# A transformer block: front loads held until x is there, roots on ScalarE, and a last tail that reads its sums from the banks

## The chip, the cores and the metric

The kernel runs on one core of a Trainium2 chip. The metric is the device time of one execution in microseconds (us); smaller is better. Engines are named as in the profile: PE (TensorE's matmuls), PEld (its weight loads), DVE (VectorE), ACT (ScalarE), POOL (GpSimd) and SP (SyncE, which issues most DMAs). A bank is one eighth of PSUM, the memory that matmuls write: 128 partitions of 512 fp32 numbers.

## The reference

One block with adaptive layer norm, for x of 2048 tokens by 512, 32 heads of 16, and an MLP of 1376; all in bf16:

```python
mod = (silu(c) @ w_mod).reshape(1, 6, 1, 512)
sa, ca, ga, sb, cb, gb = (mod[:, i] for i in range(6))
h = layernorm(x) * (1 + ca) + sa              # eps 1e-5
q, k, v = split_heads(h @ wqkv)
x = x + ga * (softmax(q @ k.T / 4) @ v merged @ wo)
h = layernorm(x) * (1 + cb) + sb
x = x + gb * (gelu(h @ w1 + b1) @ w2 + b2)
```

## The kernel before

The tokens are four blocks of 512. The attention is cut into 32 quads: quad (b, t) is four heads (t of 8) for the queries of block b. For each quad, 16 tiles of 128 keys times four heads give 64 score items, each one matmul into a bank (L949). Most go in units of three and two banks, by turns (pools psA and psB), through one exp on ACT (L1001); key tiles 3, 7, 11 and 15 go through DVE instead, as 16-bit integers whose bits are read as fp16 (L1067, L1088). The value products (`do_pv`, L1144) sum a quad in one bank (`od`, pool psO), four matmuls side by side in column groups; `do_fill` (L1165) adds products with zeros where PE would be idle. Pools ptA and ptB hold four exp results of each kind.

At a quad's end `do_out` (L1172) copies the bank to memory (`o_sb`, L1176), sends the row of sums over DRAM to `dall` and, as reciprocals (L1193), back as `rb`; POOL multiplies (L1201) and gives the tile OT. The last quad of all takes no trip: shuffle, reciprocal, multiply on DVE (L1185 to L1187).

**Front (L117 to L373).** Two DMA queues (SP and ACT) are given all loads at once: c, x of block 0 (`xb[0]`), the modulation weights W_m0, parts of W_k and W_q, the other blocks of x, W_v, the rest. `silu_c` computes silu(c); DVE takes the sums of block 0 (`ln_stats`, L201), aggregates them (L209) and finds 1/sqrt(var + eps) by shift, subtraction and two Newton rounds (`ln_rstd`, L203 to L229: nine small instructions); `ln_norm` (L232) writes the normalized rows. PE meanwhile does 13 matmuls of zeros (`warm_up`), the modulation columns (L246) and four more, then transposes (L237). `hT_evac` (L272) applies shift and scale; the first k and q products follow, and q's evacuation on DVE (L305).

**Middle.** The order of everything between is written out by a planner in the program: at each step of a planned clock every engine takes the next thing that is ready by planned durations. Side work (layer norm, projections, modulation, o-projection, MLP of finished blocks) stands in a list of jobs `job(at, rows, needs, label, hold)`: `at` is the due time in quads, `rows` are (engine, planned us, function), `needs` are labels that must have been set, and `hold` says up to which row the job keeps one of the two spare banks (pools psX0 and psX1, `aux`), which DVE's score tiles use too. Each engine executes its own instructions in the order in which the planner recorded them.

`tail_jobs(b)` (L564) is what follows attention for blocks 0 to 2: x is loaded again (`begin`), `oproj` sums eight products OT by W_o_pad in a bank (L586), DVE multiplies by ga (L592), POOL adds x (L595), then layer norm, up, gelu on ACT, down (L653), multiplication by gb and POOL's addition (L663).

**Last tail (L676 to L755).** For block 3 it starts when the attention pools are closed: eight banks `fb` for four tiles `po[tt]`, 32 products (L695), then by halves of 256 tokens `norm_half` (multiply by ga L702, add x L704 or on POOL L707, sums, `ln_rstd`, rows), `transposes`, `up_half` (44 matmuls L727, 11 gelus L729), at the end `range_flag`, one product that tells whether any softmax sum left its range (then a general path runs; not here), and four `down_tile` (L734, L736) with DVE's multiply (L739), add (L741) and the store (L742):

```python
norm_half(0)
transposes(0)
norm_half(1)
up_half(0)
transposes(1)
up_half(1)
bad, onec, fl = range_flag()
...
for tt in range(4):
    down_tile(tt)
```

Of the kernel before, what the change touches and what calls it, by code (L numbers as in the profile page):

```python
# [58 lines left out]
WARM = (13, 4)  # L59
# [30 lines left out]
def adaln_block(ctx: ExitStack, tc: tile.TileContext, A_x, A_wqkv, A_wo, B_x, B_w1, B_b1, B_w2, B_b2,  # L90
# [26 lines left out]
    wm_v = w_mod.rearrange("(j p) n -> p j n", p=P)  # L117
# [22 lines left out]
    nc.sync.dma_start(out=W_v, in_=wqkv_v[:, :, 2 * D:3 * D])  # L140
    for b in range(2, NQB):
        nc.sync.dma_start(out=xb[b], in_=x_tok[b])
    nc.sync.dma_start(out=W_k[:, :, 256:D], in_=wqkv_v[:, :, D + 256:2 * D])
    nc.sync.dma_start(out=W_q[:, :, 256:D], in_=wqkv_v[:, :, 256:D])
    W_m1 = load_mod(1, (nc.sync,))
# [18 lines left out]
    nc.vector.tensor_scalar(out=qmask, in0=pmask, scalar1=Q_SCALE, scalar2=None, op0=ALU.mult)  # L164
    magic = const.tile([P, 12], I32, name="magic")
# [64 lines left out]

    def ln_norm(src, dst, mv, rs, t, i):
        nc.vector.tensor_scalar(out=dst[:, t, :], in0=src[:, t, :], scalar1=mv[:, i, 0:1],  # L232
                                scalar2=rs[:, i:i + 1], op0=ALU.subtract, op1=ALU.mult)
# [30 lines left out]
    def second_mod_mm(ps):  # L264
        mod_cols(ps, W_m1, D, 0)
        mod_cols(ps, W_m2, 0, 4)
# [65 lines left out]
    def ln1(blocks):  # L332
        n = 4 * len(blocks)
        st = pron.tile([P, 12, 6], FP32, name="st1")
        for i in range(n):
            ln_stats(xb[blocks[i // 4]], st, i % 4, i)
        return st

    def ln1_norm(blocks, st):
        mv, rs = ln_rstd(st, 4 * len(blocks))  # L340
        for i, b in enumerate(blocks):
            for t in range(4):
                ln_norm(xb[b], xb[b], mv, rs, t, 4 * i + t)
            hn_t[b] = xb[b]

    with tc.tile_pool(name="pps", bufs=1, space=PSUM) as pps0, \
# [3 lines left out]
        st0 = ln1([0])  # L350
# [21 lines left out]
        q_proj(ps, 0, 0)  # L372
        q_evac(ps, 0, 0)  # L373
# [12 lines left out]
    NA, NB = UNIT  # L386
    att = ExitStack()
    psA = att.enter_context(tc.tile_pool(name="psA", bufs=1, space=PSUM))
    psB = att.enter_context(tc.tile_pool(name="psB", bufs=1, space=PSUM))
    psO = att.enter_context(tc.tile_pool(name="psO", bufs=1, space=PSUM))  # L390
# [5 lines left out]

    banks = [att.enter_context(tc.tile_pool(name=f"psX{i}", bufs=1, space=PSUM)) for i in range(2)]
# [20 lines left out]
    st_of = {}  # L418
# [58 lines left out]
    for b in range(1, NQB):  # L477
        at = 0.25 * (b - 1)
        def stats(j, b=b, t=0):
            if t == 0:  # L480
                st_of[b] = pron.tile([P, 12, 6], FP32, name="st1")
            ln_stats(xb[b], st_of[b], t, t)
        job(at - 0.16, [(DVE_, V_EVAC, lambda j, b=b, t=t, f=stats: f(j, b, t)) for t in range(4)],
# [23 lines left out]
    job(4.5, [(DVE_, 2.2, load_wo)], (), "wo")  # L507
# [11 lines left out]
    def row_job(at, dst, W, col0, label):  # L519
        proj_job(at, lambda ps, js: mod_row(ps, W, col0, js), lambda ps: nc.vector.tensor_copy(out=dst, in_=ps),  # L520
                 ["silu"], label)

    row_job(5.3, ga_b, W_m1, 0, "ga")
    row_job(5.5, gb_b, W_m2, D, "gb")
# [39 lines left out]
    def tail_jobs(b):  # L564
# [15 lines left out]
        def oproj(tt):  # L580
            def f(part):
                def g(j):
                    if part == 0:
                        j.ps = j.alloc()
                    for t in (2 * part, 2 * part + 1):
                        nc.tensor.matmul(out=j.ps, lhsT=OT[(b, t)][:, tt * P:(tt + 1) * P], rhs=W_o_pad[:, t, :],  # L586
                                         start=(t == 0), stop=(t == 7))
# [11 lines left out]
            job(p0 + 0.5 + 0.25 * tt, [(PE_, 2 * MM, f(i)) for i in range(4)]  # L599
                + [(DVE_, V_EVAC, mul), (POOL_, 1.2, res), (DVE_, V_EVAC, stats)],  # L600
                ["wo", ("begin", b)] + [("ot", b, t) for t in range(8)] + ([("o", b, tt - 2)] if tt > 1 else []),
# [44 lines left out]
        def down(tt):  # L646
# [18 lines left out]
            job(p0 + 4.9 + 0.5 * tt, [(PE_, (3 if i == 0 else 1 if i == 5 else 2) * MM, f(i)) for i in range(6)]  # L665
# [6 lines left out]
    for b in range(NQB - 1):  # L672
        tail_jobs(b)
    jobs.sort(key=lambda o: o.at)

    def last_tail():  # L676
# [4 lines left out]
        xr = tl.tile([P, 4, D], BF16, name="xr")  # L681
        nc.sync.dma_start(out=xr, in_=x_tok[b])
        x1 = xr
# [5 lines left out]
        with tc.tile_pool(name="fps", bufs=8, space=PSUM) as fps:  # L689
            def bank(dt=FP32, n=512):  # L690
                return fps.tile([P, n], dt, name="fb")
            po = [bank() for _ in range(4)]
            for t in range(8):
                for tt in range(4):
                    nc.tensor.matmul(out=po[tt], lhsT=OT[(b, t)][:, tt * P:(tt + 1) * P], rhs=W_o_pad[:, t, :],  # L695
                                     start=(t == 0), stop=(t == 7))
# [716 lines left out]
```

## Time and profile before

| What | Value |
|---|---|
| time, median of 3 runs | 824.18 us (823.38 to 824.9) |
| time of the profiled execution | 826.04 us |
| its span on the core | 824.3 us, 18344 instructions |
| PE busy | 781.8 us (95%), 7518 matmuls |
| DVE busy | 734.2 us (89%) |
| ACT busy | 750.6 us (91%) |
| POOL busy | 74.3 us (9%) |
| mean granted PE clock | 0.988 |
| first exp starts | 18.68 us |
| last exp ends | 778.49 us |
| last attention copy starts | 779.03 us |
| last DVE result ends | 820.24 us |

Times in the profile count from the span's start. A line of the timeline gives start, length, engine, source line, operation, result and operands with their sizes, how many instructions are merged, and in brackets how long the engine was idle before and what ended that wait. A matmul's own length (380 ns for 512 columns) is longer than the distance to the next one, since they are pipelined. A stage table gives busy times by engine in a stretch, the clock that PE was granted (1.00 is full, 0.50 half), and the share and rate of the DMA engines.

### The profile page before, as it was taken

How to read it: one execution, taken by the hardware profiler on the slowest of the kernel's cores; microseconds unless marked ns; L12 is line 12 of the kernel's file. 1: busy time of each engine (PE TensorE's matmuls, PEld its weight loads, DVE VectorE, ACT ScalarE, POOL GpSimd, SP SyncE). 2: the span in 40 equal slices, each digit the busy share in tenths (PEclk: the TensorE clock that was granted, in tenths of full speed). 3: DMA queues.
4: the chain of work that ended last, by engine and by line, in shares of the span. 5: the costliest groups of instructions: out<-in, count | busy, mean ns of one | idle time of the engine just before them, and what ended most of it. 6: DMA issues, size and time to landing. Idle time of an engine off the chain costs nothing. (4 is left out here: it accounts for less than half of the span.)

```text
span 824.3 us, 18344 instructions
## 1 busy us (share of the span) xinstructions
PE 781.8 (95%) x7518; PEld 238.0 (29%) x7518; DVE 734.2 (89%) x1324; ACT 750.6 (91%) x669; POOL 74.3 (9%) x68
## 2 busy tenths in 40 slices
PE   6999999999999999999999999999999999999967
PEld 3332222322222222222223222222223222222343
DVE  6969989999999899989989999989998999888673
ACT  2798999999999999999989999999999999999732
POOL 0000010000011000111021000011012000111010
PEclk8999999999999999999999999999999999999989
DMA  9100000113100000001100000000100000000000
GB/s 286 47 1 15 16 16 10 43 49 109 41 15 15 15 15 16 21 16 28 44 4 17 15 16 15 22 18 18 40 16 15 16 16 15 8 28 22 16 26 29
DMA packets 30667, 24.51 MB, mean 30 GB/s; under 512 B 13841, under 2 KB 24434, under 8 KB 30578
## 3 DMA queue, kind: packets, MB, share of 16 engines
q1 hardware_dynamic: 28978, 22.23, 9.5%
q8 instruction: 61, 1.00, 0.5%
q10 hardware_dynamic: 1600, 1.05, 0.4%
q14 instruction: 28, 0.23, 0.1%
HBM read 20.65 MB, written 2.61 MB: 28 GB/s over the span
## 5 line engine op out<-in xcount | busy, mean ns | idle before, releaser
L1001 ACT ACTIVATE pA<-sA 128x1536 bf16<-128x1536 f32 x310 | 467.1, 1507 | 16.0 <-PE od L1144 8.2
L1067 DVE TENSOR_SCALAR t<-aux 128x512 int16<-128x512 f32 x500 | 329.1, 682 | 29.0 <-PE aux L949 27.2
L1001 ACT ACTIVATE pB<-sB 128x1024 bf16<-128x1024 f32 x309 | 335.1, 1084 | 5.7 <-PE sB L949 2.5
L1088 DVE TENSOR_SCALAR t<-t 128x2048 int16<-128x2048 int16 x375 | 263.6, 725 | 2.1 <-PE od L1144 0.5
L949 PE MATMUL aux<-qm,kT 32*128 32x512 bf16 x500 | 175.2, 380 | 4.1 <-DVE t L1067 2.1
L949 PEld LDWEIGHTS <-kT 32*128 32x128 bf16 x2048 | 77.2, 91 | 270.6 <-issue 265.2
L1144 PE MATMUL od<-pA,VE 128*32 128x512 bf16 x930 | 143.3, 385 | 0.2 <-DVE o_sb L1176 0.2
L1144 PE MATMUL od<-pB,VE 128*32 128x512 bf16 x618 | 142.3, 386 | 0.0
L1144 PE MATMUL od<-t,VV 128*32 128x512 f16 x1500 | 139.4, 385 | 1.4 <-DVE t L1088 1.0
L949 PE MATMUL sA<-qm,kT 32*128 32x512 bf16 x930 | 123.2, 383 | 11.0 <-ACT pA L1001 8.6
L949 PE MATMUL sB<-qm,kT 32*128 32x512 bf16 x618 | 120.7, 383 | 2.9 <-ACT pB L1001 2.5
L1201 POOL TENSOR_TENSOR OT<-o_sb,rb 128x512 bf16<-128x512 f32 x31 | 41.3, 1332 | 526.1 <-DMA rb<-d 354.2
L1165 PE MATMUL od<-hT,zeros 128*32 128x512 bf16 x940 | 83.1, 385 | 0.0
L1144 PEld LDWEIGHTS <-VE 128*32 128x32 bf16 x2048 | 50.7, 94 | 98.1 <-issue 85.0
L1144 PEld LDWEIGHTS <-VV 128*32 128x32 bf16 x1500 | 39.9, 95 | 55.7 <-issue 46.9
L1144 PE MATMUL od<-t,VE 128*32 128x512 f16 x500 | 49.2, 384 | 1.3 <-DVE o_sb L1176 1.2
L628 PE MATMUL aux<-h2T,W 128*128 128x512 bf16 x132 | 39.7, 384 | 0.8 <-DVE t L1067 0.7
L653 PE MATMUL aux<-W,uG 128*128 128x512 bf16 x132 | 37.7, 383 | 0.0
L1165 PEld LDWEIGHTS <-zeros 128*32 128x32 bf16 x972 | 23.9, 95 | 36.4 <-issue 29.2
L1176 DVE COPY o_sb<-od 128x512 f32<-128x512 f32 x32 | 21.9, 684 | 8.0 <-issue 7.6
L633 DVE TENSOR_SCALAR uG<-aux,b1c 128x512 bf16<-128x512 f32 x33 | 24.4, 739 | 2.7 <-PE aux L628 2.6
L586 PE MATMUL aux<-W_o_pad,OT 128*128 128x512 bf16 x96 | 26.4, 382 | 0.2 <-DVE t L1067 0.2
(128 smaller groups left out, 417.3 us busy)
## 6 DMA issues: line engine op xcount, KB each, us to landing
rb<-d SPq DMA_DIRECT2D x124, 64.0 KB
W_m<-in_w_mod_dram SPq DMA_DIRECT2D x2, 1024.0 KB
xr<-in_A_x_dram SPq DMA_DIRECT2D x4, 512.0 KB
out_dram<-ob SPq DMA_DIRECT2D x16, 128.0 KB
xb<-in_A_x_dram SPq DMA_DIRECT2D x3, 512.0 KB
W<-in_B_w_dram SPq DMA_DIRECT2D x1, 1376.0 KB
W<-in_B_w_dram SPq DMA_DIRECT2D x1, 1280.0 KB
W_m<-in_w_mod_dram SPq DMA_DIRECT2D x1, 512.0 KB
```

The lines of the kernel that those rows point to most:

```text
L586: nc.tensor.matmul(out=j.ps, lhsT=OT[(b, t)][:, tt * P:(tt + 1) * P], rhs=W_o_pad[:, t, :], start=(t == 0), stop=(t == 7))
L628: nc.tensor.matmul(out=j.ps, lhsT=late["W_1"][:, c, fc * P:(fc + 1) * P], rhs=T["h2"][:, c, :], start=(c == 0), stop=(c == NC - 1))
L633: nc.vector.tensor_scalar(out=T["u"][:, fc, :], in0=j.ps, scalar1=late["b1c"][:, fc:fc + 1], scalar2=None, op0=ALU.add)
L653: nc.tensor.matmul(out=j.ps, lhsT=T["u"][:, fc, tt * P:(tt + 1) * P], rhs=late["W_2"][:, fc, :], start=False, stop=(fc == NFC - 1))
L949: nc.tensor.matmul(out=dst, lhsT=kT[32 * r:32 * r + 32, ch, kt * P:(kt + 1) * P], rhs=qm[(b, ch)][32 * r:32 * r + 32, par, :], start=True, ...
L1001: nc.scalar.activation(out=pt[:, 0:n, :], in_=st[:, 0:n, :], func=ACT.Exp, scale=math.log(2.0) / STEP)
L1067: nc.vector.tensor_scalar(out=t0[(qi, kt)][:, r, :], in0=sd, scalar1=T_BIAS, scalar2=0.0, op0=ALU.add, op1=ALU.max)
L1088: nc.vector.tensor_scalar(out=t16, in0=t0[(qi, kt)], scalar1=float(MJ[j]), scalar2=None, op0=ALU.add)
L1144: nc.tensor.matmul(out=od[qi][32 * r:32 * r + 32, :], lhsT=w, rhs=src, start=first, stop=last_)
L1165: nc.tensor.matmul(out=dst[32 * r:32 * r + 32, :], lhsT=zeros, rhs=hT[:, r, 0:512], start=bank is not None, stop=bank is not None)
L1176: nc.vector.tensor_copy(out=o, in_=od[qi])
L1201: nc.gpsimd.tensor_tensor(out=OT[(b, t)], in0=o, in1=j.rb, op=ALU.mult)
```

## The change

Four things, in the words of the code.

1. Front. x and c are loaded first, c and W_m0 with neighbouring rows in one partition; W_m0 follows. All other loads move to `later_loads`, on SP's queue alone. It is called after the first of block 0's sums and begins with a one-element memset of W_k on DVE: the load of W_k, and all behind it in SP's queue, wait for that memset. The root for block 0 is taken by ACT (`ln_sqrt`) and inverted by DVE; an exp of one column after it brings ACT's exp table back. `warm_up` has 18 matmuls ahead of the modulation and none behind. Three of the four sums of block 1 are taken ahead of q's evacuation.
2. Residual and ga. W_o_pad is multiplied by ga once, on POOL, in eight pieces. The o-projection of blocks 0 to 2 begins with a product of the identity and x, which adds the residual in the bank; DVE then copies the sum. The multiplication by ga and POOL's addition go. The due times of the down products are 0.6 apart instead of 0.5.
3. End of attention. The last quad's shuffle, reciprocal and multiply read the bank, and the copy that feeds the range check comes behind them. The last block's x is loaded before the end, and the o-projection of its first two tiles, up to the seventh of eight products, is made by two jobs that hold both spare banks, once DVE's score tiles are done (`d_done`).
4. Last tail. Only five banks (those of psA and psB) are taken anew; the others are used where they are. Filler matmuls (5 and 18) stand around the last products. Sums are taken from the banks, ACT copies them to x1, the first half's root is ACT's; tables are loaded by one-column instructions (`early`); `down_tile(0)` moves ahead of `up_half(1)`; the last down tile is made and stored in two halves.

The same, cut (unchanged parts and the renaming that follows from it left out):

```diff
-WARM = (13, 4)
+ST1 = 3
+WARM = 18
+KEEP = (5, 18)
...
-    wm_v = w_mod.rearrange("(j p) n -> p j n", p=P)
+    wm_v = w_mod.rearrange("(p j) n -> p j n", p=P)
...
-    nc.scalar.dma_start(out=cc_bf, in_=c.rearrange("o (j p) -> p (o j)", p=P))
     for k, eng in enumerate(two):
         eng.dma_start(out=xb[0][:, 2 * k:2 * k + 2, :], in_=x_tok[0][:, 2 * k:2 * k + 2, :])
+    nc.scalar.dma_start(out=cc_bf, in_=c.rearrange("o (p j) -> p (o j)", j=NC))
     W_m0 = load_mod(0, two)
-    nc.sync.dma_start(out=W_k[:, :, 0:256], in_=wqkv_v[:, :, D:D + 256])
-    nc.scalar.dma_start(out=W_q[:, :, 0:256], in_=wqkv_v[:, :, 0:256])
-    nc.sync.dma_start(out=xb[1], in_=x_tok[1])
...
+    def later_loads():
+        nc.vector.memset(W_k[0:1, 0, 0:1], 0.0)
+        nc.sync.dma_start(out=W_k[:, :, 0:256], in_=wqkv_v[:, :, D:D + 256])
+        nc.sync.dma_start(out=W_q[:, :, 0:256], in_=wqkv_v[:, :, 0:256])
+        nc.sync.dma_start(out=xb[1], in_=x_tok[1])
+        nc.sync.dma_start(out=W_v, in_=wqkv_v[:, :, 2 * D:3 * D])
...
+        mods[1] = load_mod(1, (nc.sync,))
...
+    def ln_sqrt(st, n):
+        mv = small.tile([P, 12, 2], FP32, name="mv")
+        for t in range(n):
+            nc.vector.bn_aggr(out=mv[:, t, :], in_=st[:, t, :])
+        rs = small.tile([P, 12], FP32, name="rs")
+        nc.scalar.activation(out=rs[:, 0:n], in_=mv[:, 0:n, 1], func=ACT.Sqrt, bias=eps_c)
+        nc.vector.reciprocal(out=rs[:, 0:n], in_=rs[:, 0:n])
+        return mv, rs
...
+    def ln1_norm(b, st):
+        mv, rs = ln_sqrt(st, 4)
+        nc.scalar.activation(out=ce_x, in_=eps_c, func=ACT.Exp)
+        for t in range(4):
+            ln_norm(xb[b], xb[b], mv, rs, t, t)
...
+        for t in range(4):
+            ln_stats(xb[0], st0, t, t)
+            if t == 0:
+                later_loads()
...
-        warm_up(WARM[0])
+        warm_up(WARM)
         psm = pps0.tile([P, 16], FP32, name="psm")
-        ln1_norm([0], st0)
+        ln1_norm(0, st0)
         pt_ = [ppst.tile([P, 2, 512], BF16, name="ptr") for _ in range(2)]
         first_mod_mm(psm)
-        warm_up(WARM[1])
...
         q_proj(ps, 0, 0)
+        st1 = pron.tile([P, 12, 6], FP32, name="st1")
+        for t in range(ST1):
+            ln_stats(xb[1], st1, t, t)
         q_evac(ps, 0, 0)
...
+    def scale_wo(t):
+        nc.gpsimd.tensor_tensor(out=W_o_pad[:, t, :], in0=W_o_pad[:, t, :], in1=ga_b, op=ALU.mult)
...
+    for t in range(8):
+        job(6.0 + 0.2 * t, [(POOL_, 1.2, lambda j, t=t: scale_wo(t))], ["wo_in", "ga"], ("wo", t))
...
                     if part == 0:
                         j.ps = j.alloc()
+                        nc.tensor.matmul(out=j.ps, lhsT=ident, rhs=T["xr"][:, tt, :], start=True, stop=False)
...
-            def mul(j):
-                j.tmp = late["tl2"].tile([P, D], FP32, name="tmp")
-                nc.vector.tensor_tensor(out=j.tmp, in0=j.ps, in1=ga_b, op=ALU.mult)
-
             def res(j):
-                nc.gpsimd.tensor_tensor(out=T["x1"][:, tt, :], in0=j.tmp, in1=T["xr"][:, tt, :], op=ALU.add)
+                nc.vector.tensor_copy(out=T["x1"][:, tt, :], in_=j.ps)
...
-            job(p0 + 4.9 + 0.5 * tt, [(PE_, (3 if i == 0 else 1 if i == 5 else 2) * MM, f(i)) for i in range(6)]
+            job(p0 + 4.9 + 0.6 * tt, [(PE_, (3 if i == 0 else 1 if i == 5 else 2) * MM, f(i)) for i in range(6)]
...
+    job(8 * NQB - 1.2, [(SP_, 3.0, last_begin)], [("tail", NQB - 2)], "last")
...
+    def o_mm(ps, tt, t):
+        if t == 0:
+            nc.tensor.matmul(out=ps, lhsT=ident, rhs=last["xr"][:, tt, :], start=True, stop=False)
+        nc.tensor.matmul(out=ps, lhsT=OT[(NQB - 1, t)][:, tt * P:(tt + 1) * P], rhs=W_o_pad[:, t, :],
+                         start=False, stop=(t == 7))
...
+        job(8 * NQB - 1.0 + 0.05 * tt, [(PE_, n * MM, f(i)) for i, n in enumerate((3, 2, 2, 1))],
+            ["last", "d_done"] + [("ot", NQB - 1, t) for t in range(7)], ("last", tt), 99)
...
-        with tc.tile_pool(name="fps", bufs=8, space=PSUM) as fps:
+        with tc.tile_pool(name="fps", bufs=5, space=PSUM) as fps:
+            own = [(fps, "fb"), (psO, "od"), (banks[0], "aux"), (banks[1], "aux")] + [(fps, "fb")] * 4
...
+            nc.scalar.activation(out=early, in_=eps_c, func=ACT.Sqrt)
+            po = [last[0], last[1], bank(), bank()]
+            for tt in (2, 3):
+                for t in range(7):
+                    o_mm(po[tt], tt, t)
+            idle = bank()
+            def keep_on(n):
+                for _ in range(n):
+                    nc.tensor.matmul(out=idle, lhsT=ident, rhs=hT[:, 0, 0:512], start=True, stop=True)
+            keep_on(KEEP[0])
+            for tt in range(4):
+                o_mm(po[tt], tt, 7)
+            keep_on(KEEP[1])
...
             def norm_half(hf):
                 tts = (2 * hf, 2 * hf + 1)
...
+                    nc.vector.bn_stats(out=st[:, tt, :], in_=po[tt])
+                    nc.scalar.copy(out=x1[:, tt, :], in_=po[tt])
+                mv, rs = (ln_rstd if hf else ln_sqrt)(st[:, 2 * hf:2 * hf + 2, :], 2)
...
             norm_half(0)
+            nc.scalar.activation(out=early, in_=b1c[:, 0:1], func=ACT.Gelu_apprx_tanh)
             transposes(0)
             norm_half(1)
             up_half(0)
             transposes(1)
+            down_tile(0)
             up_half(1)
...
-            for tt in range(4):
+            for tt in (1, 2):
                 down_tile(tt)
+            down_tile(3, 2)
...
         b, t = quads[qi]
+        if qi == nq - 1:
+            rb = odp.tile([P, 512], FP32, name="rb")
+            nc.vector.stream_shuffle(out=rb, in_=od[qi], mask=[16] * 32)
+            nc.vector.reciprocal(out=rb, in_=rb)
+            ot = otp.tile([P, 512], BF16, name="OT")
+            OT[(b, t)] = ot
+            nc.vector.tensor_tensor(out=ot, in0=od[qi], in1=rb, op=ALU.mult)
         o = odp.tile([P, 512], FP32, name="o_sb")
         nc.vector.tensor_copy(out=o, in_=od[qi])
...
+        if not d_tiles and not d_items:
+            lab.setdefault("d_done", clock)
```

More of the change, by code (lines that the diff above doesn't have):

```diff
@@ L330, in adaln_block @@
     hn_t = [None] * NQB
[L332 to L344, printed above, removed]
+    def ln1_norm(b, st):
[3 more added lines that the diff above has]
+            ln_norm(xb[b], xb[b], mv, rs, t, t)
+        hn_t[b] = xb[b]
     with tc.tile_pool(name="pps", bufs=1, space=PSUM) as pps0, \
@@ L386, in adaln_block @@
     NA, NB = UNIT
+    bk = ExitStack()
+    banks = [bk.enter_context(tc.tile_pool(name=f"psX{i}", bufs=1, space=PSUM)) for i in range(2)]
+    psO = bk.enter_context(tc.tile_pool(name="psO", bufs=1, space=PSUM))
     att = ExitStack()
@@ L395, in adaln_block @@
     tp = att.enter_context(tc.tile_pool(name="tp", bufs=T_BUFS))
-    banks = [att.enter_context(tc.tile_pool(name=f"psX{i}", bufs=1, space=PSUM)) for i in range(2)]
     lab = {}
@@ L680, in last_tail @@
         W_1, W_2, b1c = late["W_1"], late["W_2"], late["b1c"]
-        xr = tl.tile([P, 4, D], BF16, name="xr")
-        nc.sync.dma_start(out=xr, in_=x_tok[b])
-        x1 = xr
+        x1 = last["xr"]
         h2 = tl.tile([P, NC, 512], BF16, name="h2T")
@@ L688, in last_tail @@
         st = tl.tile([P, 4, 6], FP32, name="st2")
-        with tc.tile_pool(name="fps", bufs=8, space=PSUM) as fps:
+        with tc.tile_pool(name="fps", bufs=5, space=PSUM) as fps:
+            own = [(fps, "fb"), (psO, "od"), (banks[0], "aux"), (banks[1], "aux")] + [(fps, "fb")] * 4
+            turn = [0, 0, 0] + [1, 2, 3, 0]
             def bank(dt=FP32, n=512):
-                return fps.tile([P, n], dt, name="fb")
-            po = [bank() for _ in range(4)]
-            for t in range(8):
-                for tt in range(4):
-                    nc.tensor.matmul(out=po[tt], lhsT=OT[(b, t)][:, tt * P:(tt + 1) * P], rhs=W_o_pad[:, t, :],
-                                     start=(t == 0), stop=(t == 7))
+                if not turn:
+                    turn.extend(range(8))
+                pool, nm = own[turn.pop(0)]
+                return pool.tile([P, n], dt, name=nm)
+            early = tl.tile([P, 1], FP32, name="early")
+            nc.scalar.activation(out=early, in_=eps_c, func=ACT.Sqrt)
[11 more added lines that the diff above has]
+            keep_on(KEEP[1])
@@ L1376, in adaln_block @@
     last_tail()
+    bk.close()
     general_path()
```

100 lines of the change are left out of this document (49 added, 51 removed).

## The prediction

> **What bounds the kernel now.** I read the table of stages first (busy us of each engine), then the timeline at both ends, the clock in fine stretches, and ScalarE's waits.
>
> ```profile
> 300.00:400.00 100.00, 98.49 (x963) 28.28 (x962) 93.60 (x154) 99.11 (x85) 11.67 (x9) 1.00 0.08 24
> ...
> 779.00:825.00 46.00, 32.42 (x189) 17.93 (x185) 26.67 (x61) 11.86 (x25) 2.27 (x2) 0.89 0.08 25
> ```
>
> Columns: stretch, length, busy PE, PEld, DVE, ACT, POOL, then clock, DMA share, GB/s. Between 18.7 and 778.5 us ACT's exps are the bound (99.11 of 100 us). They number 619 before and after, so this stage changes only by ACT's idle time. Ahead of the first exp and behind the last one nothing is full: these 18.7 and 45.8 us are chains of waits, and there the change acts.
>
> ```profile
> 11.10 1.38 DVE L232 TENSOR_SCALAR xb<-xb,mv,rs 128x512 bf16<-128x512 bf16 x4
> ...
> 12.68 1.91 PE L237 MATMUL ptr<-ident,xb 128*128 128x128 bf16 x16
> ...
> 17.38 1.41 DVE L305 TENSOR_SCALAR qm<-ppj,qmask 128x512 bf16<-128x512 f32 x2 [2.19 <-PE ppj L296]
> ...
> 18.68 1.45 ACT L1001 ACTIVATE pA<-sA 128x1536 bf16<-128x1536 f32 x1 [1.58 <-PE sA L949]
> ```
>
> The front: DVE's rows are normalized 1.82 us after the aggregation's end (9.28), which tiny steps fill; transposes start when both the rows (12.48) and four warm-up matmuls are over.
>
> ```profile
> 779.87 7.07 PE L695 MATMUL fb<-W_o_pad,OT 128*128 128x512 bf16 x32 [0.72 <-DVE o_sb L1176]
> 793.14 1.25 PE L237 MATMUL fb<-ident,hnL 128*128 128x128 bf16 x8 [6.21 <-DVE hnL L232]
> 794.26 6.81 PE L727 MATMUL fb<-h2T,W 128*128 128x256 bf16 x44
> 800.90 0.84 PE L237 MATMUL fb<-ident,hnL 128*128 128x128 bf16 x8
> 801.92 5.26 PE L727 MATMUL fb<-h2T,W 128*128 128x256 bf16 x41 [0.17 <-DVE h2T L277]
> ```
>
> PE in the tail: it waits 6.2 us for DVE, then about 1.0 and 1.1 us for transposed rows. The long wait costs the clock as well:
>
> ```profile
> 10.00:12.00 2.00, 1.79 (x33) 1.23 (x34) 1.79 (x9) 0.00 (x0) 0.00 (x0) 0.50 1.11 330
> ...
> 791.00:792.00 1.00, 0.00 (x0) 0.00 (x0) 0.83 (x6) 0.00 (x0) 0.00 (x0) 0.50 0.00 0
> ...
> 796.00:798.00 2.00, 2.00 (x12) 1.40 (x11) 1.03 (x2) 1.99 (x4) 1.63 (x2) 0.54 0.03 8
> ```
>
> Clock 0.50 from 791 to about 797, and at the front from 9.4 to 16 (0.84 in 8 to 10).
>
> **Tail, counted from the last attention copy's start (779.03 = T).**
> - DVE: shuffle 0.72, reciprocal 3.35, multiply 0.69 and their 0.04 gaps start at T, without the copy: OT at T+4.85 (before T+5.6). Shuffle and multiply now read a bank; copies from a bank take 0.68, like those from memory: ends 0.1 either way.
> - PE: tiles 0 and 1 have 14 of 16 products before the last exp. Behind it stand 2 residual products, 14 more and 5 fillers, 21 x 0.2165 (the pitch of 512-wide matmuls) = T+4.5, under the reciprocal. Then 4 products to T+5.8 and 18 fillers to T+9.7.
> - DVE: the copy, now behind OT, to T+5.5; sums over two banks (0.69 each, row of L201; from a bank unseen, 0.6 to 0.75) T+6.8; aggregation T+7.1. ACT's copies (0.59, row of L288) end T+7.45, its root T+7.7 (0.21, the 128x4 exp; unseen, 0.15 to 0.8); reciprocal 0.18; rows T+8.4 and T+8.7 (before T+14.4). The fillers end 1 us later, so **PE sets the pace**.
> - PE from T+9.7: 8 transposes 0.65, 0.85 until ACT's second evacuation, 41 matmuls 4.64 (their time from 802.87 on, clock 1.00): T+15.85. DVE's second half (evacuations T+10.8, sums T+12.1, Newton steps 2.1 and rows 0.75 as before: T+15.0) hides behind that with 0.85 to spare; past it PE waits one for one. Transposes 0.65; down tile 0 (2.8) covers the evacuations that cost 1.1; 44 matmuls 4.97; flag 0.1; two down tiles 5.6; the halved one 2 x 1.4: T+32.8. DVE's multiply and add of 256 columns, 0.4 each (128x256 row of L277): T+33.65, before T+41.2. What follows (820.24 to 824.3) stays 4.06; a store half as large could save tenths, none taken. **Gain 7.6**, bounds 5.5 to 8.3.
>
> ACT's gelu table load follows the root: 7.7 + 0.49 + 1.28 (idle and length of the load at 795.57) = T+9.5, before the evacuation at T+10.15 wants it. The Trainium skill ("ScalarE: Activation LUTs", What ACT_TABLE_LOAD costs) adds a drain of about 1.38 us to every switch. By it ACT would be free at T+10.9 and the gain an estimated 0.7 less; against it, the first gelu at 796.86 starts as the load ends.
>
> **Front.** x and W_m0 (1.5 MB) come first; at the 345 GB/s of 8 to 16 us both are there by 8.1 (W_m0 before: 10.2). DVE waits for c ahead of its sums; c landed at 5.13 in 512 pieces sent first, now in 128 behind x: 4.5 to 6.5, taken 5.5. Sums 6.2 to 8.85, aggregation 9.25, root 9.6, reciprocal 9.9, rows 11.3. Eighteen warm-ups (8 at 0.43, 10 at 0.21) end at 8.3, modulation at 9.3. Transposes end 12.4, ACT's evacuations (0.78 each) 13.6, q's products 14.7 at full clock.
>
> The memset on W_k lets SP's queue, W_q's part from ACT's queue included, go on at 7.1 only: W_k, W_q and xb[1] are 1 MB, from 9.1 (2 us as at the start) at 345 GB/s 12.2. DVE's three sums of xb[1], ahead of q's evacuation, want it at 12.9 and fill its idle 2.2 us. So the cover is 0.7 us; past that, q, the first scores and all exps wait one for one. W_v follows at 13.7, wanted at 16.5.
>
> Clock: it fell at 9.4 after 1.2 busy us since 6.0. Between modulation and keys PE does only 1.3 us of transposes, so I take it to fall again; the last key product and four of q's then cost 5 x 0.215 = 1.1 more. First exp 17.3 against 18.68: **gain 1.4** (2.5 at full clock). The early chain has three sums less, but the next key copy now stands behind six Newton steps on DVE: gain 0.3.
>
> **Middle.** PE gets 12 residual products and 16 of the last block (28 x 0.2165 = 6.1) and loses 25 groups of zero fillers (0.21 each, 5.3). DVE's copies (0.685) replace multiplies (0.680); POOL loses 12 adds (14.2 us) and gets 8 scalings (1.24 each, the row of L663: 9.9) that nobody waits for until the first o-projection at 233. The order matters more. An exp needs the buffer that the value products of eight units earlier free. In PE's order before, five units have those behind the next unit's scores, by 1.88, 1.11, 0.21, 0.11 and 0.05 us of PE work; the trace's stalls there are 3.02, 2.85, 0.87, 0.87, 0.85. In the new order 1.11 and 0.11 stay, the rest goes (-4.74), and 0.48, 0.11, 0.27, 0.31, 0.64 come; at work + 0.75 that is 5.56. **Loss 0.8**, between -4.7 and +6.
>
> **Sum.** -7.6 - 1.4 - 0.3 + 0.8 = -8.5. The profiled execution took 826.04 (span 824.3 and 1.74 around it), 1.86 above the median 824.18 of the runs. Forecast 817.5 for it, **815.7** for the median. 0.2% (1.65 us) is about what a measurement can tell from no change.
>
> **Rivals.**
> - Clock kept at the front: 1.1 less, 814.6. For it: PE's longest gap is 1 us, and half of the modulation's time may count. The Trainium skill ("TensorE: Matmul & The Clock Gate", Part 1) has the clock fall after an idle window of about 3.4 us. By that rule it is kept; against it, here it fell 1.7 us after the last matmul at 7.7.
> - The new stalls are absorbed, the old ones gone: 5.5 less, 810.2. For it: three stand close together.
> - More stalls: each of three blocks meets one like 428 and 435 us (3.89): 11.7 - 4.7 = 7.0 instead of 0.8, 821.9. For it: each o-projected tile has one product more.
> - The gate is late: xb[1] at 14.4, 1.5 more, 817.2. DMA share is 1.1 from 6 to 22 us, so nothing can be made up.
> - It does not do what it says: tail clock 0.50 all the same, 18 fillers 7.8, up matmuls 2.3 more: tail gain 1.4, 821.9. Against it: no PE gap over 0.4 us.
> - **Slower**: PE's products of the last block stand ahead of the last units' scores and need OT of quad 30, whose trip SP now sends behind the last x (512 KB, 3 us at the 177 GB/s of 784 to 786). OT came at 770.9 and is wanted at 775.1; its trip took 13.7. Each us beyond 4.2 delays the last exps one for one: from 14.3 more, a doubled trip, it is slower by 0.2%; at 15 more 826.5. Against: x goes out 3.5 us ahead.
>
> **Chances.** Forecast 0.42 (own range 813.5 to 817.5), clock kept 0.20, stalls absorbed 0.09, more stalls 0.10, late gate 0.10, tail clock 0.04, slower 0.03, no effect 0.02. The range 810.0 to 820.0 leaves out the dear ones (0.19). Faster 0.95, same 0.02, slower 0.03.
>
> **What would show it.** Right: first exp near 17.3; the last tail's transposes 9.7 us after the shuffle's start, clock 1.00 from there; no idle PE between the halves; last result 33.7 after it. Wrong: DVE idle ahead of the sums of xb[1], ACT's waits on od over 13 us, PE waiting for OT of quad 30.

## The result and the profile after

| | before | changed |
|---|---|---|
| time, median of 4 runs beside each other | 823.94 us (823.38 to 824.9) | 816.78 us (815.8 to 818.05) |
| ratio, 95% interval | | 0.9913 [0.9894, 0.9931] |
| profiled execution | 826.04 (span 824.3) | 815.8 (span 814.0) |
| first exp starts | 18.68 | 17.31 |
| 13th exp starts | 42.02 | 39.48 |
| last exp starts | 777.00 | 773.82 |
| T, start of the last copy (before) or shuffle (after) | 779.03 | 776.02 |
| from T to the span's end | 45.27 | 37.98 |

The change saves 7.2 us by the medians. The two profiled executions differ by 10.2, since that of before took 2.1 more than the median of these runs, and that of after 1.0 less; so I read lengths of stages from them, and totals from the ratios.

Stages of the changed kernel (columns as before: busy PE, PEld, DVE, ACT, POOL, clock, DMA share, GB/s):

```profile
6.00:8.00 2.00, 2.00 (x6) 0.76 (x5) 1.87 (x7) 1.31 (x2) 0.00 (x0) 1.00 0.31 118
8.00:10.00 2.00, 2.00 (x31) 1.15 (x30) 1.60 (x8) 0.62 (x2) 0.00 (x0) 1.00 0.66 199
10.00:12.00 2.00, 1.68 (x29) 1.19 (x26) 1.59 (x7) 1.16 (x2) 0.00 (x0) 1.00 1.00 262
...
300.00:400.00 100.00, 96.53 (x940) 27.56 (x947) 91.85 (x154) 99.60 (x85) 12.22 (x9) 1.00 0.09 23
776.00:814.00 38.00, 31.56 (x205) 19.06 (x206) 21.29 (x49) 14.66 (x33) 0.00 (x0) 0.95 0.05 16
```

The middle is as full of exps as it was (99.60 of 100). The last stage is 7.3 us shorter with nearly the same PE work. New is the hole that the gate makes in the DMA share from 6 to 10 us.

The timeline of the front:

```profile
9.90 1.38 DVE L253 TENSOR_SCALAR xb<-xb,mv,rs 128x512 bf16<-128x512 bf16 x4
10.37 1.87 PE L258 MATMUL ptr<-ident,xb 128*128 128x128 bf16 x16
...
13.49 1.88 DVE L213 BATCH_NORM_STATS2 st<-xb 128x6 f32<-128x512 bf16 x3 [0.66 <-DMA xb<-in_A_x_dram]
15.28 1.40 DVE L326 TENSOR_SCALAR qm<-ppj,qmask 128x512 bf16<-128x512 f32 x2
16.82 0.39 PE L1019 MATMUL sA<-qm,kT 32*128 32x512 bf16 x3 [1.67 <-DVE qm L326]
17.31 1.45 ACT L1071 ACTIVATE pA<-sA 128x1536 bf16<-128x1536 f32 x1 [2.40 <-DVE st L213]
```

The rows come 1.2 us earlier than before. But DVE waits 0.66 us for x of block 1, which the prediction names as a sign of being wrong, and the first scores start at 16.82, after both halves of q's evacuation (15.28 to 16.68); before, they started 0.8 us after its start.

PE and its helpers in the tail:

```profile
781.79 4.05 PE L764 MATMUL fb<-hT,ident 128*128 128x512 bf16 x18
783.18 0.30 ACT L248 ACTIVATE rs<-mv,eps_c 128x2 f32<-128x2 f32 x1
783.50 1.28 ACT L813 ACT_TABLE_LOAD   x1
783.51 0.17 DVE L249 RECIPROCAL rs<-rs 128x2 f32<-128x2 f32 x1 [0.63 <-ACT rs L248]
784.79 0.20 ACT L813 ACTIVATE early<-b1c 128x1 f32<-128x1 f32 x1
785.68 0.28 PE L258 MATMUL od<-ident,hnL 128*128 128x128 bf16 x2
...
791.65 0.28 PE L258 MATMUL aux<-ident,hnL 128*128 128x128 bf16 x2
```

The 6.2 us without work ahead of the first transposes are gone, and from T on PE goes through to the second ones with no wait over 0.41 us, at clock 1.00.

### The profile page after: what moved, and what is told of

It reads as the page before. It is cut to its first block, busy times and chain, and to the rows that moved or that the text cites. A ratio compares the mean times of both kernels' runs of the same rounds, so it can differ in the third digit from the quotient of the medians.

```text
span 814.0 us, 18164 instructions
## 1 busy us (share of the span) xinstructions
PE 771.9 (95%) x7404; PEld 237.5 (29%) x7470; DVE 723.8 (89%) x1306; ACT 756.2 (93%) x681; POOL 71.2 (9%) x62
## 4 chain that ended last, share of the span: by engine, by line
PE 46%; ACT 24%; DVE 17%; issue 10%; DMA 2%; SPq 0%; POOL 0%; ACTq 0%; DVEq 0%; POOLq 0%
PE od L1214 14%; ACT pA L1071 14%; ACT pB L1071 9%; DVE t L1137 7%; PE sA L1019 6%; PE sB L1019 6%; DVE t L1158 6%; PE aux L1019 4%; PE aux L678 3%; PE od L1235 2%; PE aux L615 2%; PE aux L653 2%; PE aux L303 1%; PE fb L805 1%; PE aux L317 1%
## 5 line engine op out<-in xcount | busy, mean ns | idle before, releaser
L1071 ACT ACTIVATE pA<-sA 128x1536 bf16<-128x1536 f32 x310 | 469.1, 1513 | 16.3 <-PE od L1214 7.2
L1158 DVE TENSOR_SCALAR t<-t 128x2048 int16<-128x2048 int16 x375 | 260.1, 715 | 2.6 <-PE od L1214 1.4
L1019 PE MATMUL aux<-qm,kT 32*128 32x512 bf16 x500 | 177.5, 380 | 6.2 <-DVE t L1137 3.4
L1272 POOL TENSOR_TENSOR OT<-o_sb,rb 128x512 bf16<-128x512 f32 x31 | 43.2, 1394 | 559.3 <-DMA rb<-d 288.4
L1235 PE MATMUL od<-hT,zeros 128*32 128x512 bf16 x844 | 76.0, 385 | 0.0
L678 PE MATMUL aux<-W,uG 128*128 128x512 bf16 x120 | 35.5, 383 | 1.6 <-issue 1.6
L653 PE MATMUL aux<-h2T,W 128*128 128x512 bf16 x113 | 35.6, 384 | 0.5 <-issue 0.3
L1235 PEld LDWEIGHTS <-zeros 128*32 128x32 bf16 x872 | 21.8, 95 | 36.1 <-issue 30.6
L688 POOL TENSOR_TENSOR ob<-tmp,xr 128x512 bf16<-128x512 f32 x12 | 15.7, 1305 | 115.1 <-DVE tmp L684 115.1
```

Source lines behind the costliest of these rows:

```text
L653: nc.tensor.matmul(out=j.ps, lhsT=late["W_1"][:, c, fc * P:(fc + 1) * P], rhs=T["h2"][:, c, :], start=(c == 0), stop=(c == NC - 1))
L678: nc.tensor.matmul(out=j.ps, lhsT=T["u"][:, fc, tt * P:(tt + 1) * P], rhs=late["W_2"][:, fc, :], start=False, stop=(fc == NFC - 1))
L688: nc.gpsimd.tensor_tensor(out=o, in0=j.tmp, in1=T["x1"][:, tt, :], op=ALU.add)
L1019: nc.tensor.matmul(out=dst, lhsT=kT[32 * r:32 * r + 32, ch, kt * P:(kt + 1) * P], rhs=qm[(b, ch)][32 * r:32 * r + 32, par, :], start=True, ...
L1071: nc.scalar.activation(out=pt[:, 0:n, :], in_=st[:, 0:n, :], func=ACT.Exp, scale=math.log(2.0) / STEP)
L1158: nc.vector.tensor_scalar(out=t16, in0=t0[(qi, kt)], scalar1=float(MJ[j]), scalar2=None, op0=ALU.add)
```

## The experiments

All ratios are to runs of before, made beside the kernel in question. "Same orders" means that every engine has its instructions in the changed kernel's order.

| kernel | ratio, 95% interval | first exp | 13th exp | T to end |
|---|---|---|---|---|
| changed | 0.9913 [0.9894, 0.9931] | 17.31 | 39.48 | 37.98 |
| 1 old tail | 1.0019 [0.9999, 1.004] | 17.91 | 41.00 | 45.46 |
| 2 scalings of one column | 0.9893 [0.9877, 0.991] | 17.81 | 41.28 | 37.63 |
| 3 q's bank | 0.9931 [0.9903, 0.9958] | 17.26 | 39.42 | 37.73 |
| 4 no fillers | 0.9941 [0.9917, 0.9964] | 18.53 | 41.96 | 37.25 |
| 5 no gate | 0.9931 [0.9906, 0.9955] | 17.33 | 39.49 | 37.85 |
| 6 pools | 0.992 [0.9885, 0.9955] | 17.82 | 40.24 | 37.67 |
| 7 fewer fillers | 0.9913 [0.9894, 0.9932] | 17.17 | 39.34 | 36.68 |
| 8 scaling on DVE, own plan | 0.9968 [0.9954, 0.9982] | 18.30 | 40.46 | 37.70 |
| 9 scaling on DVE, same plan | 0.9886 [0.9856, 0.9915] | 18.40 | 40.56 | 37.67 |
| 10 = 5 + 6 + 7 | 0.9885 [0.9856, 0.9914] | 16.41 | 38.58 | 36.53 |
| 11 = 10 + 9 | 0.9852 [0.9824, 0.988] | 16.33 | 38.49 | 36.68 |
| 12 = 11, other due times | 0.9866 [0.9834, 0.9899] | 17.56 | 39.72 | 36.60 |

By these intervals a total tells edits apart only from some 0.3% (2.5 us) on; below that the profiles' stages decide.

**1. The old tail.** My theory was that the tail gives the gain; the rival, that the middle does.

```diff
-        if qi == nq - 1:
-            rb = odp.tile([P, 512], FP32, name="rb")
...
-    job(8 * NQB - 1.2, [(SP_, 3.0, last_begin)], [("tail", NQB - 2)], "last")
+                    nc.vector.tensor_scalar(out=tmp, in0=po[tt], scalar1=1.0, scalar2=None, op0=ALU.mult)
...
```

> The changed kernel with the last tail of before put back (x loaded late, copy ahead of shuffle, multiply and add on DVE and POOL, Newton roots, four whole down tiles last, no fillers); W_o stays scaled, so the multiply is by 1.0, an operation of the same length. Every engine's order up to the last quad is that of the changed kernel. Theory (the tail gives 7.3 of the gain, the rest comes from front and middle): last shuffle or copy at the same time as in the changed kernel within 0.5 us, from the copy's start to the end 45.3 us as before, time 816.8 + 7.3 = 824.1. Rival (the two tails are about equal and the gain is the middle's): under 819.

Measured: 1.0019, from T to the end 45.46. With the old tail, PE of this kernel waits again:

```profile
793.06 1.25 PE L258 MATMUL fb<-ident,hnL 128*128 128x128 bf16 x8 [6.21 <-DVE hnL L253]
```

The ratio is 0.0106 above the changed kernel's, 8.7 us (about 2.3 either way, by the two intervals). So the tail (parts 3 and 4 of the change) holds all of the gain, and everything else together is worth between nothing and 3 us of loss (1.0019 [0.9999, 1.004]). The rival falls. One thing was not as expected: the last copy starts at 778.94, 2.9 us after T of the changed kernel instead of within 0.5, though the orders are the same. Of that, 1.5 us are there at the 13th exp (41.00) and 3.2 at the 157th (217.95 against 214.80); the clock fell in this execution at 17, 177 and 208 us. Which piece of the tail gives how much was not tested apart, but for the fillers.

**2. Scalings of one column.** This answers to a pattern that I had not forecast. Between 165 and 215 us the changed kernel's ACT is busy 45.81 of 50 us; before it was 49.54. POOL's scalings stand there:

```profile
168.88 3.85 POOL L406 TENSOR_TENSOR W_o_pad<-W_o_pad,ga_b 128x512 bf16<-128x512 bf16 x3 [4.34 <-DVE ga_b L548]
170.22 3.07 DVE L1158 TENSOR_SCALAR t<-t 128x2048 int16<-128x2048 int16 x2
175.50 1.45 ACT L1071 ACTIVATE pA<-sA 128x1536 bf16<-128x1536 f32 x1 [1.25 <-PE sA L1019]
```

Two shifts, 0.68 each elsewhere, take 3.07 while POOL scales (a single one at most 1.65, not the 1.85 that I name below); DVE is late with its score tiles, PE with the next scores, and ACT idles 1.25.

```diff
-        nc.gpsimd.tensor_tensor(out=W_o_pad[:, t, :], in0=W_o_pad[:, t, :], in1=ga_b, op=ALU.mult)
+        nc.gpsimd.tensor_tensor(out=W_o_pad[:, t, 0:1], in0=W_o_pad[:, t, 0:1], in1=ga_b[:, 0:1], op=ALU.mult)
```

> Each of POOL's eight scalings of W_o_pad is cut to one column (511 of 512 columns stay unscaled, so ga is left out there); all orders are the same. Theory (a scaling on POOL holds up DVE's 128x2048 shifts, which reach 1.85 us instead of 0.68, and the exps then wait for scores): the ACT gaps at 174 (1.25), 178 (1.37) and 204 to 208 us (1.4) go, 4.0 together; the exp near 215 us starts 3.5 to 4 earlier than in the changed kernel, and at the end 2 to 4 are left: 813 to 815. Rival (the shifts are late for another reason, or later stages take it all back): within 0.8 of 816.8.

Measured: ACT busy 49.57 of those 50 us. From the 13th to the 157th exp it takes 171.4 us instead of 175.3, so 3.9 us are gained. But 2.3 of them are lost by 229: after a wait of 0.77 us PE runs at half clock.

```profile
219.02 0.53 PE L1214 MATMUL od<-t,VE 128*32 128x512 f16 x4 [0.77 <-DVE o_sb L1253]
...
219.00:226.00 7.00, 6.98 (x54) 1.27 (x53) 4.77 (x8) 5.14 (x5) 0.00 (x0) 0.51 0.03 5
```

By the last exp nothing of the gain is left in this execution (735.2 us from the 13th on, 734.3 in the changed kernel's), and the median, 815.66, lies between the theory's 813 to 815 and the rival's 816.0 and more. So the cause of the stalls is shown; what it is worth at the end is not.

**3 and 6. The first scores.** The rows of the front showed them waiting for both halves of q's evacuation. I took the bank for the cause, first q's alone, then the pool's.

```diff
+        ppsm.tile([P, 512], FP32, name="ppj")
         ps = ppsm.tile([P, 512], FP32, name="ppj")
         q_proj(ps, 0, 0)
```

> One more bank is taken from the front's pool ahead of q's, so that q's products no longer lie in a bank that the first scores want. Same orders. Theory (the first scores waited for both halves of q's evacuation because they overwrite its bank): scores start after the first half, 16.1 instead of 16.8, first exp at 16.6 instead of 17.3, time 816.1. Rival (they wait for the other half for its data, or for the queue): first exp stays at 17.3, time 816.8.

Measured: no change, the wait is 1.67 as in the changed kernel. So I took a pool to give its banks back as one, and the four banks of the projections' pool still reached into those of psA. (Before opened psA first, on the banks of the modulation and the transposes; the change opens the two spare banks and psO ahead of it.) The next try moved the pool:

```diff
-    with tc.tile_pool(name="pps", bufs=1, space=PSUM) as pps0, \
-            tc.tile_pool(name="ppst", bufs=2, space=PSUM) as ppst, \
-            tc.tile_pool(name="ppsm", bufs=4, space=PSUM) as ppsm:
+    with tc.tile_pool(name="ppsm", bufs=3, space=PSUM) as ppsm, \
+            tc.tile_pool(name="pps", bufs=1, space=PSUM) as pps0, \
+            tc.tile_pool(name="ppst", bufs=2, space=PSUM) as ppst:
```

> The front's three bank pools are opened in another order (projections first, three banks instead of four), so that the first score unit's banks were those of the transposes and not of the projections. Same orders on every engine. Theory (moving only q's bank changed nothing because the whole pool is given back at once; with its banks elsewhere the first scores wait for q's first half alone): scores start some 0.7 us before q's second half ends, at 16.1, first exp 16.6; PE's wait is 1.0 instead of 1.7, so the clock falls less often; time 816.0. Rival (the wait is for the data, or what is gained is lost at the next wait): first exp 17.3, or exp 13 still at 39.4; 816.8.

```profile
16.51 1.41 DVE L326 TENSOR_SCALAR qm<-ppj,qmask 128x512 bf16<-128x512 f32 x2 [0.48 <-PE ppj L317]
17.31 0.39 PE L1019 MATMUL sA<-qm,kT 32*128 32x512 bf16 x3 [0.84 <-DVE qm L326]
...
14.00:16.00 2.00, 2.00 (x6) 0.59 (x4) 1.85 (x3) 0.59 (x1) 0.00 (x0) 0.50 1.08 360
```

The scores now start 0.8 after the evacuation does, and PE waits 0.84: the pool was it. But the first exp came at 17.82, not at the 16.6 that I expected, and the median was 819.37, not 816.0: in this execution x of block 1 came 1.24 us late, and the clock fell to 0.50 under q's products (1.9 us instead of 1.0). Runs 10 and 11 show the gain, below.

**5. The gate.**

```diff
-        nc.vector.memset(W_k[0:1, 0, 0:1], 0.0)
```

> The memset of W_k that holds SP's later loads is left out; nothing else moves. Theory (the gate makes xb[1] late, and whether PE then waits 1.7 or over 1.9 us for q decides if its clock falls): the DMA share keeps over 0.9 from 6 to 10 us instead of 0.23 to 0.8; DVE's sums of xb[1] start at 12.9 behind its rows of hT, with no wait for a DMA (0.66 to 1.91 in the runs with the gate); q is evacuated from 15.1; no clock below 1.00 between 12 and 22 us; the first exp at 17.1; time 815.8 or a little less, with a smaller spread. Rival (the gate pays: without it W_m0 or x come later): the modulation's end past 10.4 or the aggregation past 9.4, first exp 17.8 or later, time 817.5.

```profile
6.00:8.00 2.00, 2.00 (x8) 0.83 (x7) 1.76 (x6) 1.42 (x2) 0.00 (x0) 1.00 1.07 363
8.00:10.00 2.00, 1.72 (x37) 1.16 (x35) 1.60 (x8) 0.53 (x2) 0.00 (x0) 1.00 1.10 375
...
12.84 1.87 DVE L213 BATCH_NORM_STATS2 st<-xb 128x6 f32<-128x512 bf16 x3
```

The hole in the DMA share is filled, x of block 1 is there without a wait, and nothing comes later for it: the sums of block 0 start at 6.67 (6.39 to 6.81 in the profiles with the gate), the modulation ends at 9.7. First exp 17.33, 0.2 later than I expected and as in the best executions with the gate. So the gate gives nothing here, and with it x of block 1 comes late by an uneven amount: DVE waited 0.60 to 1.91 us for it in nine profiles. The time is not the 815.8 of the theory: 818.98, ratio 0.9931, is no better than with the gate, and the spread (5.4 us) is no smaller. The profile has two falls of the clock, at 205 and 273 us, where the edit does not reach. Nor is the gate what lets the clock fall at the front: run 12 has none, and its clock fell at 13.5 us.

**4 and 7. Fillers of the tail.**

```diff
-KEEP = (5, 18)
+KEEP = (0, 0)
```

> The 23 filler matmuls of the last tail are left out. Theory (they keep the clock): transposes start at T+8.5 instead of T+9.7 (T: start of the last shuffle), but the clock falls to 0.50 in the 2.6 us without work, the up products take 0.215 instead of 0.11 each for 3 us or more: 1.2 gained, 3 lost, 818.6. Rival (the idle time is too short for the clock to fall): clock 1.00 throughout, the gain is kept, 815.6.

Without any, transposes start at T + 8.25, and the clock falls, but for 3.4 us only:

```profile
786.00:788.00 2.00, 0.70 (x6) 0.57 (x7) 1.03 (x4) 1.97 (x4) 0.00 (x0) 0.75 0.04 4
788.00:790.00 2.00, 2.00 (x13) 1.25 (x11) 1.98 (x6) 1.69 (x5) 0.00 (x0) 0.50 0.00 0
790.00:792.00 2.00, 2.00 (x18) 1.71 (x17) 1.59 (x10) 2.00 (x6) 0.00 (x0) 0.89 0.00 0
```

From T to the end 37.25, shorter than with 18. Both theories fall by half: the clock does fall, and that costs less than the fillers do. (The median, 818.31, is near the theory's 818.6 by luck: the tail did not lose what the theory said, and the profiled execution has the latest front of all.)

```diff
-KEEP = (5, 18)
+KEEP = (5, 13)
```

> The last tail has 5 + 13 filler matmuls instead of 5 + 18. Theory (the fillers outlast the rows by 1.1 us, and with 13 PE still has no gap over 0.3 us): transposes at T+8.5 instead of T+9.66, clock 1.00, from T to the end 36.9 instead of 37.7 to 38.0; DVE's second half then is the next limit and takes back some 0.3. Time 815.9. Rival (the clock falls as without fillers): half rate from T+8 for 3.4 us, from T to the end 37.3 as without any.

Measured: transposes at 786.10, T + 8.58, clock 1.00, 36.68 from T to the end: 1.0 to 1.3 less than in the kernels with 18 (37.63 to 37.98). The total (816.95, ratio 0.9913) does not show it; it is less than a total tells.

**8 and 9. Scaling on DVE.**

```diff
-    ga_b = res.tile([P, D], FP32, name="ga_b")
+    ga_b = res.tile([P, D], BF16, name="ga_b")
...
-        nc.gpsimd.tensor_tensor(out=W_o_pad[:, t, :], in0=W_o_pad[:, t, :], in1=ga_b, op=ALU.mult)
+        nc.vector.tensor_tensor(out=W_o_pad[:, t, :], in0=W_o_pad[:, t, :], in1=ga_b, op=ALU.mult)
...
-        job(6.0 + 0.2 * t, [(POOL_, 1.2, lambda j, t=t: scale_wo(t))], ["wo_in", "ga"], ("wo", t))
+        job(6.0 + 0.2 * t, [(DVE_, 0.35, lambda j, t=t: scale_wo(t))], ["wo_in", "ga"], ("wo", t))
```

> W_o_pad is scaled by DVE, with ga in bf16, in eight operations of 0.35 to 0.7 us; the planner moves other work for that, so orders differ from the second quad on. Theory (POOL's scalings cost the exps 2.6 to 4.6 us between 170 and 215, by DVE's blocked shifts and the clock that falls behind them): with no 1.2 us operation to wait for, shifts in that stretch take 0.68 but for those beside POOL's OT products; ACT's gaps between 165 and 215 are under 1.5 together; time 814. Rival (DVE is full there, so 3 to 5 us more work on it costs as much, or another plan brings its own waits): 816 to 819.

> The planner's rows stay as they are (POOL, 1.2 us), but the eight scalings are given to DVE (ga in bf16, 0.42 us each as measured in the run with its own plan): the other instructions keep the changed kernel's order on every engine. Theory (the gaps of 170 to 215 us come from 1.2 us scalings on the port that DVE's shifts need, the rest of that run's time from its other plan): ACT's gaps between 165 and 215 fall from 2.6 to 4.6 to under 1.5, no clock below 1.00 between 165 and 215, the o-projection's gaps after 240 stay as they are (1.77, 0.99, 0.35, 1.25); time 814.0 to 815.5. Rival (3.3 us more on a DVE that is full cost the same): gaps over 2.5 in that stretch, 816.8 or more.

Run 9 leaves out the last edit, the planner's row. In both, ACT's idle time from 165 to 215 us is down (0.82 and 1.34 of 50 us) and the clock stays at 1.00. DVE's groups in the changed kernel, then in run 9, from 165 to 210 us (count, then busy us and the mean ns of one, then idle us):

```profile
L1158 DVE TENSOR_SCALAR t<-t 128x2048 int16<-128x2048 int16 x24 | 20.5, 873 | 0.1
```

```profile
L1158 DVE TENSOR_SCALAR t<-t 128x2048 int16<-128x2048 int16 x25 | 17.5, 711 | 0.1
...
L406 DVE TENSOR_TENSOR W_o_pad<-W_o_pad,ga_b 128x512 bf16<-128x512 bf16 x8 | 3.3, 414 | 0.0
```

DVE pays 3.3 us for the scalings itself, and the shifts give back 873 - 711 ns, 24 times: 3.9 us. With the plan kept, the time is 0.9886 (814.99, in the theory's range). That interval overlaps the changed kernel's, but the 732.6 us from the 13th to the last exp are less than in any of the seven profiles with the scaling on POOL and the same plan (734.3 to 739.5). With its own plan (run 8) it is 0.9968: the new order brings gaps of 2.20 at 270, 3.48 at 502, 2.21 at 622 and 2.05 at 625 us, all behind value products. There the rival was right.

**10, 11 and 12. Together.** Run 10 is the edits of 5, 6 and 7, run 11 adds that of 9, run 12 these:

```diff
-            job(p0 + 0.5 + 0.25 * tt,
+            job(p0 + 0.5 + 0.5 * tt,
...
-            job(p0 + 4.9 + 0.6 * tt,
+            job(p0 + 4.9 + 0.7 * tt,
```

> Gate off, bank pools in the other order, 5 + 13 fillers, together; orders of the changed kernel. Theory (each mends one thing that its own profile showed, and they are on different stretches): first scores 0.1 after q's first half, first exp 16.5 to 16.7; from the last shuffle to the end 36.7; no clock below 1.00 ahead of 160 us. Against the changed kernel 0.7 + 1.1 and, in those of its executions whose clock fell at the front, 0.8 to 1.7 more: 814.5. Rival (what the front gains is lost at the next wait for DVE): exp 13 at 39.4 as before, 815.7.

> The same with the scalings on DVE in the planner's old places. Theory: the gains add: 814.5 less 1.5 to 3 is 811.5 to 813. Rival (what the middle gains is given back at the next fixed wait, as in the run with scalings of one column): within 1 us of the run without this edit.

> The same again, with the due times of the o-projection's tiles 0.5 quads apart (0.25) and of the down products' 0.7 (0.6); this is another plan from the second block on. Theory (the prediction's rule: an exp stalls where, in PE's order, the value products of eight units earlier stand behind the next unit's scores, by that work + 0.75 us): the order has such places at units 32 (1.11), 51 (0.11), 243 (0.64) and 396 (0.58), none at 180 to 185 and 339; so ACT's gaps behind value products are 2.85, 0.87, about 1.4 and 1.3, and the 4.3 at 243 to 253 and 1.7 at 437 are gone: 2.8 less than without, 809 to 810.5. Rival (the rule tells the places but new plans meet other waits, as on the run with scalings in its own plan): 812 or more.

The front of run 11:

```profile
15.03 1.41 DVE L326 TENSOR_SCALAR qm<-ppj,qmask 128x512 bf16<-128x512 f32 x2 [0.57 <-PE ppj L317]
15.83 0.39 PE L1019 MATMUL sA<-qm,kT 32*128 32x512 bf16 x3 [0.84 <-DVE qm L326]
16.33 1.45 ACT L1071 ACTIVATE pA<-sA 128x1536 bf16<-128x1536 f32 x1 [1.58 <-PE sA L1019]
```

First exp at 16.3 to 16.4 in runs 10 and 11, and the 0.9 us are still there at the 13th, so the rival of run 10 is refuted; the tails are 36.5 to 36.7. Run 12 has the same front, but in its profile the clock fell at 13.5 us, and the first exp came at 17.56. Run 10's median, 815.33, is 0.8 over the 814.5 forecast. Run 11 takes 812.72 us against 825.43 of before beside it: 0.9852 [0.9824, 0.988], faster than the changed kernel (the intervals do not meet) and in the forecast range, and its six runs lie within 1.6 us. Run 12 tests the prediction's rule for stalls. The two new places that the rule named (priced 1.4 and 1.3) stood there, and those at 243 to 253 and 437 us were gone:

```profile
314.47 1.02 ACT L1071 ACTIVATE pB<-sB 128x1024 bf16<-128x1024 f32 x1 [1.84 <-PE od L1214]
...
499.85 1.45 ACT L1071 ACTIVATE pA<-sA 128x1536 bf16<-128x1536 f32 x1 [1.67 <-PE od L1214]
```

But gaps of 0.34, 0.48, 1.30 and 0.72 at 299, 301, 396 and 574 us came that it had not named, and its time, 813.2 (0.9866), is not below that of run 11 and not the 809 to 810.5 of the theory; the rival was right. The rule tells where a plan stalls; it does not tell what a new plan costs in all.

## Why the prediction was right, step by step

815.7 was forecast for the median, 816.78 measured. The tail was right in size and in mechanism. The front came out at the forecast time by luck, and the middle has a cost that I put at nothing. The terms, each against what the runs show:

- **Tail, gain 7.6:** 45.27 less 37.98 is 7.3 in the profile of after; six other kernels with the same tail (2, 3, 5, 6, 8, 9) need 37.63 to 37.85, which is 7.4 to 7.6 less than before. Transposes came at T + 9.66 (forecast 9.7), the last result at T + 33.5 (33.65), and what follows took 4.5 instead of 4.06. That the fillers set the pace was right, and run 7 shows that this was 1 us given away. Gelu's table load begins 0.02 us after the root (783.18 + 0.30), and ACT's next instruction starts as the load ends (783.50 + 1.28, 784.79). So the drain that the Trainium skill ("ScalarE: Activation LUTs", What ACT_TABLE_LOAD costs) adds to each switch is not to be seen here.
- **Front, gain 1.4, and early chain, 0.3:** 17.31 was forecast to 0.01, but by luck, not by its steps. The clock did not fall (1.1 less), x of block 1 came 0.6 late, and the pool's wait (0.7) was not in my list, though the new order of the bank pools is part of the change. (I also counted 1.2 busy us of PE ahead of the fall in before; the profile's row has 1.45.) First exps came from 17.17 to 18.53 in nine profiles with the gate (median 17.82; all but runs 3 and 6 have the same front), and in six of them the clock fell to 0.50 between 12 and 22 us. The 13th exp, with everything early in it, started at 39.34 to 41.96 in the eight of them with the old pools, median 40.51: a gain of 1.5 over the one profile of before, against the 1.7 of the two terms. So the size held for a typical execution, and "clock kept" and "gate late" were not rivals of which one is true: both differ from one execution to the next.
- **Middle, loss 0.8:** from the 13th to the last exp it took 734.98 before and 734.3 to 739.5 in the seven executions that have the changed kernel's scaling and plan (changed, 1, 3, 4, 5, 6, 7), median 735.98: a loss of 1.0 (in the changed kernel's own profile a gain of 0.6). The stalls behind value products that were to go (3.02, 0.87, 0.85) went. Of the five that were to come, four came, at 244.6, 247.9, 253.3 and 438.4 us, and one did not; those at 250.6 and 623.0 were not on the list:

```profile
244.56 1.45 ACT L1071 ACTIVATE pA<-sA 128x1536 bf16<-128x1536 f32 x1 [1.76 <-PE od L1214]
247.92 1.45 ACT L1071 ACTIVATE pA<-sA 128x1536 bf16<-128x1536 f32 x1 [0.99 <-PE od L1214]
250.63 1.45 ACT L1071 ACTIVATE pA<-sA 128x1536 bf16<-128x1536 f32 x1 [0.35 <-PE od L1214]
253.33 1.02 ACT L1071 ACTIVATE pB<-sB 128x1024 bf16<-128x1024 f32 x1 [1.25 <-PE od L1214]
438.39 1.02 ACT L1071 ACTIVATE pB<-sB 128x1024 bf16<-128x1024 f32 x1 [1.74 <-PE od L1214]
622.96 1.45 ACT L1071 ACTIVATE pA<-sA 128x1536 bf16<-128x1536 f32 x1 [0.81 <-PE od L1214]
```

Together they are 6.9 in place of 5.56.
- **Front and middle against runs:** taken from one profile of before, which was 2.1 us over its median, these gains are probably too large. Run 1 has no such doubt: without the tail, the change is worth nothing or a little less (the forecast's terms for these parts: 0.9 gained). If it is worth nothing, this and the tail's 0.3 are the 1.1 us by which the median was missed; the runs are too uneven to tell the two apart.
- **The step that failed** is in the middle's term: eight scalings on POOL "that nobody waits for". They cost ACT 4.2 to 7.6 us of idle time between 165 and 215 us in eight executions, against 0.5 before. They use no busy engine, but a shift of DVE's that meets one takes up to 0.97 us more. Runs 2 and 9 show it: with scalings of one column, or on DVE, these gaps go. The Trainium skill says so ("SBUF — State Buffer", Who interferes with whom): DVE in its two-port modes and POOL use one port pair, and whoever comes second is blocked for the whole instruction. The rows agree: beside scalings single shifts of the changed kernel took up to 1.65 us, which is their usual 0.685 and 0.97 more, less than the length of one scaling (1.16 to 1.62). The net loss stayed small because other gaps went: those over 0.25 us that lie outside of 165 to 215 us and are not put down to value products (`od`) sum to 5.6 us before and 2.3 after, from the 13th exp on. I did not test where they went: POOL's 12 additions, beside which shifts of before were long as well (1.65 us at 237.7), are gone too, and the orders are new.
- **The rivals:** the slower one is refuted: POOL gives OT of quad 30 at 770.3, and PE's products of the last block, from 770.4 on, waited for nothing.

```profile
769.00 1.28 POOL L1272 TENSOR_TENSOR OT<-o_sb,rb 128x512 bf16<-128x512 f32 x1 [11.79 <-DMA rb<-d]
```

"Tail clock 0.50" is refuted, and so are "stalls absorbed" and "more stalls" (ACT's waits behind value products came to 11.1 us in all, under the 13 that were to show it).

## What to carry to other kernels

Undo the largest part alone: here one run showed that the tail held the whole gain, and it was the part that could be counted from rows, as a chain. An engine with idle time is not free: ask what it shares with the bound one before work is moved onto it. Here the fillers that keep the clock did best when they ended as the data came, and a gate or an order of pools at the start is checked by what the first instruction behind it waits for.

## What the hardware showed

In these fourteen profiles the granted clock fell to 0.50 for about 3.4 or 6.8 us, never for another length (but for the last fall of most, which the span's end cuts). From rows of 1 us, as twice the clock that is missing in them: 3.42 from 175 us on in the changed kernel, 6.82 from 204 in run 3, 6.84 from 219 in run 2, 3.40 from 787 in run 4, 6.82 from 9 in before. The Trainium skill ("TensorE: Matmul & The Clock Gate", Part 1) has a free-running window of 3413 ns, which fits these lengths, and fits that the same instructions meet a fall in one execution and none in the next. It has the clock fall after an idle window; here much less sufficed: in 3.4 us just ahead of the fall (in run 2 the row takes in its first 0.25 us) PE was busy 2.63 in run 2 and 2.22 in the changed kernel:

```profile
216.00:219.40 3.40, 2.63 (x25) 0.77 (x24) 3.40 (x6) 3.36 (x4) 0.00 (x0) 0.96 0.00 0
```

```profile
171.80:175.20 3.40, 2.22 (x30) 0.53 (x23) 3.40 (x5) 2.45 (x3) 0.94 (x1) 1.00 0.00 0
```

These falls are a part of the spread of the runs. Of run 6's seven, the three over 821 us had a mean granted clock of 0.984 to 0.989, the four below 820 one of 0.993 to 0.996; of run 12's six, the two over 815 had 0.992 and 0.993, the four below 814 had 0.996 to 0.999. They are not its only cause: the six of run 7 (815.97 to 818.76) show no such order, and the slowest of them had the highest clock, 0.996.
